# Four of w_out's eight pieces requested behind the store of w_sp's halves, and converted behind the last theta

## The chip, the cores and the metric

The kernel runs on one core of one Trainium2 chip. The metric is the device time of one execution in microseconds (us), lower is better. Times shown as "median of runs" are of repeated executions; a profiled execution is a further one, from which all rows of the trace come.

## The reference, cut to what matters

Three blocks follow one another on an activation of 4 batches x 576 positions x 512 channels, all in float32:

```python
# 1. windowed attention, 8 heads: softmax(scale * q k^T + mask) v           -> x [4, 576, 512]
# 2. mixing
theta = x @ w_theta                                  # 512 x 512
zr, zi = x * cos(theta), x * sin(theta)
u = x + w_tok_r @ zr + w_tok_i @ zi                  # over the 576 positions
x2 = u + relu(u @ w_ch)
# 3. gated MLP
h = relu(x2 @ w_in); hu, hv = h[..., :512], h[..., 512:]
v_s = w_spatial @ layernorm(hv) + b_spatial          # over the 576 positions
out = (hu * v_s) @ w_out                             # w_out is 512 x 512
```

The weights are handed in as float64; products are made in pairs of float32r numbers ("h" and "l", the rounded value and the rest), so each weight must be converted and split before it is used. `w_out` is needed by the last product only.

## The kernel before, in words

TensorE (PE) holds three matmuls for every product (h with h, l with h, h with l). Work is staged by batch: attention of batch b+1 and the mixing of batch b run side by side, then the gated MLP runs batch by batch. The names used below:

- `th_run(3, ...)` is theta of the last batch (its sines on ScalarE (ACT), its products on VectorE (DVE), its split `zl` on GpSimd (POOL)). `tm_run(b, ks)` is the token mixing of a batch; each of its eight steps ends in a DVE addition at line 553, which is kept in the list `mixed`; `uh` and `ul` are its split sums (ACT and POOL). `ch_run(b)` is the product with `w_ch`; it ends each group in a DVE operation at line 574, which frees a PSUM bank, and in a store `x2d<-x`.
- Float64 weights arrive in pieces in the ring `w64` of the pool `stg`, which has four slots. A piece of 256 columns is converted by five instructions: ACT line 141 (`w64g<-w`), DVE line 142 (`c<-w`, into the PSUM tile `c64`), DVE line 143, the rounded half by DVE line 120 (`parts<-w64g`) and the rest by POOL line 176. Lines 141 and 142 are the last to read the slot. SyncE (SP) then stores the pair to a DRAM buffer with line 177.
- `j_out` lists w_out's eight pieces (load with line 170, conversion as above, store to `wo_d`). `wo_load` reads all of them back (line 822) for the output products.
- `w_gate(0)` and `w_gate(1)` load two pieces of `w_sp` each (lines 757 and 758) into the same ring, take **two more slots of it** for sums (`c` from line 761 on, `d` from line 764 on), and split four tiles (ACT line 767, DVE line 768). They are called `a`, `b`, `c` and `d` in the text, and `a'` to `d'` in the second call.
- `w_half()` converts the last 64 rows of `w_sp` and ends in the two stores at line 244 (`wh_d<-wsph`).
- `first_parts` (line 731) splits sums of batch 0's activation on ACT and POOL (`x2tl<-first,x2th`); `x2s`, and lines 859 to 868, are the first steps of the MLP.

The order of the work is made by a planner before the run. It walks through a modelled timeline; whenever an engine is free, it takes, of the instructions whose inputs are planned and whose tile can have a slot, the one that stands first in the program. Loads are instructions of SP's queue for it. Each engine then runs its list in that order, waiting at each instruction for its inputs. `tc.issue_after(ins)` says that what is traced inside may only stand behind `ins` on the engine of `ins`; it holds back nothing on other engines, and it makes no wait. `behind(list, f)` does that for each instruction of a list. `late(pairs, lag, last)` requests a piece per step, and lets the conversion follow two steps later, behind `last()`:

```python
def late(pairs, lag, last):
    ...
            load, finish = todo.pop(0)
            waiting.append((finish, load()))
        if len(waiting) > lag or not todo:
            finish, st = waiting.pop(0)
            behind(last(), lambda: finish(st))
```

So a load of `late` is held by nothing, and a conversion by the step of the token mixing at which it is called (on DVE, since `mixed` holds DVE instructions). Before the change all eight pieces of `j_out` run through it, spread over `tm_run(3, K_ALL)` at 1.25 calls per step: conversions are called at steps 3, 4, 4, 5, 6, 7, 8 and 8. At the same place the second half of `w_gate(0)` is called at step 4, and the loads and the second half of `w_gate(1)` at steps 5 and 6.

Of the kernel before, what the change touches and what calls it, by code (L numbers as in the profile page):

```python
# [47 lines left out]
LAG_W = 2  # L48
SECOND_RATE = 1.5
OUT_RATE = 1.25  # L50
CH_BEFORE = 4
PE_MASK = 1
PAIR = 2
HELD = 2
SP_FIRST = 5


# [7 lines left out]
K_ALL = (8,) + K_MAIN  # L65
# [3 lines left out]
def tile_block(ctx: ExitStack, tc: tile.TileContext, qT, kT, vw, eye_in, mask_in, eye_b_in, w_theta, w_tok, w_ch, w_in, w_sp, w_sph, b_sp, w_out, out):  # L69
    nc = tc.nc  # L70
    V, A, G, PE, SY = nc.vector, nc.scalar, nc.gpsimd, nc.tensor, nc.sync

    def f32(ap):
        return ap.bitcast(F32)
# [18 lines left out]
    wh_d = dram.tile([P, 2, 3 * CH], F32R, name="wh_d")  # L93
# [102 lines left out]
    def gate_half(kk):  # L196
# [14 lines left out]
        def add(blk, x, y, z, op):  # L211
            def finish(_):
                V.tensor_tensor(g[x], g[y], g[z], op=op)
                out(blk, g[x])
            return (lambda: None), finish
# [2 lines left out]
        return [read(0, 0, 0), read(1, 0, None), read(0, 1, 1), read(1, 1, 2),  # L218
                add(3, a22, a21, a22, ALU.add), add(5, a21, a11, a21, ALU.subtract), add(4, a11, a22, a11, ALU.subtract), add(6, a12, a12, a11, ALU.subtract)]

    def w_half():
        (st, bt), (hh, lb) = ([patt.tile(sh, d, tag=t, name="wsph", bufs=2) for _ in range(2)] for sh, d, t in (([P, S + WIN], F32, "k"), ([P, NT, P], F32R, "v")))
        hh, lb = (t.rearrange("p t k -> p (t k)")[:, :3 * CH] for t in (hh, lb))
        sd = stg.tile([P, CH], F32, tag="stage", name="stage", bufs=4)
        bd = stg.tile([P, CH], F32, tag="stage", name="stage", bufs=4)

        def load():
            SY.dma_start(st[:, :S], w_sph)
            for r in (64, 96):
                SY.dma_start(bt[r:r + 1, :S], b_sp)  # L230

        def finish(_):
            V.tensor_tensor(sd, st[:, :CH], st[:, CH:S], op=ALU.subtract)
            G.memset(f32(lb[HALF:]), 0.0)
            for r in (64, 96):
                V.tensor_tensor(bd[r:r + 1], bt[r:r + 1, :CH], bt[r:r + 1, CH:S], op=ALU.subtract)
            for s_, b_, c in ((st[:, :S], bt[:, :S], slice(0, S)), (sd, bd, slice(S, 3 * CH))):
                A.copy(hh[:, c], s_)
                V.tensor_tensor(lb[:HALF, c], s_[:HALF], f32(hh[:HALF, c]), op=ALU.subtract)
                for r in (64, 96):  # L240
                    A.copy(lb[r:r + 1, c], b_[r:r + 1])
                V.tensor_tensor(lb[96:97, c], b_[96:97], f32(lb[96:97, c]), op=ALU.subtract)
            for i, t in enumerate((hh, lb)):
                SY.dma_start(f32(wh_d[:, i]), f32(t))

        return load, finish

# [188 lines left out]
    zlast = {}  # L436
    x_cast = []
    mixed = []
# [3 lines left out]
    def split(dst_h, dst_l, src, eh="a", el="g"):  # L442
        copy(dst_h, src, eh)
        return (G if el == "g" else V).tensor_tensor(dst_l, src, f32(dst_h), op=ALU.subtract)  # L444
# [68 lines left out]
    def th_shared(b):  # L513
        th_unit(b, 4, True)
        yield

    def th_run(b, ts):
        for t in ts:
            th_unit(b, t)
            yield  # L520

    def u_tiles(b):
        if b not in uu:
            uu[b] = tuple(p1.tile([P, 4, S], F32R, tag=n, name=n) for n in ("uh", "ul"))
        return uu[b]

    def tm_run(b, ks, last=True):

        if last:
            uh, ul = u_tiles(b)  # L530
        for c in range(2):
            cs = slice(CH * c, CH * (c + 1))

            early = b == 0 and c == 0
            accs = []
            for d in range(4):
                if early and d < 2:
                    if d == 0:
                        accs = [ps_mm.tile([P, 512], F32, tag="mm", name="ps_y") for _ in range(2)]
                        for i, k in enumerate(ks):  # L540
                            for e in range(2):
                                for j, (lh, rh) in enumerate(((zh, wtok_h), (zl, wtok_h), (zh, wtok_l))):
                                    PE.matmul(accs[e][:, :CH], lh[b, k][:, P * e:P * (e + 1)], rh[:, k, cs], start=(i + j == 0), stop=(i == len(ks) - 1 and j == 2))
                    ps = accs[d]
                else:
                    ps = ps_mm.tile([P, 512], F32, tag="mm", name="ps_y")
                    n = 0
                    for k in ks:
                        for lh, rh in ((zh, wtok_h), (zl, wtok_h), (zh, wtok_l)):
                            PE.matmul(ps[:, :CH], lh[b, k][:, P * d:P * (d + 1)], rh[:, k, cs], start=(n == 0), stop=(n == 3 * len(ks) - 1))  # L550
                            n += 1
                xv = x[b][:, d, cs]
                mixed.append(V.tensor_tensor(xv, ps[:, :CH], xv, op=ALU.add))
                if last:
                    x_cast.append(split(uh[:, d, cs], ul[:, d, cs], xv, "a", "g"))
                yield
# [3 lines left out]
    def ch_run(b):  # L560

        uh, ul = uu.pop(b)
        wch_h, wch_l = wch
        for c in range(2):
            cs = slice(CH * c, CH * (c + 1))
            for e in range(4):
                ps = ps_mm.tile([P, 512], F32, tag="mm", name="ps_r")
                n = 0
                for k in range(4):
                    for lh, rh in ((wch_h, uh), (wch_l, uh), (wch_h, ul)):  # L570
                        PE.matmul(ps[:, :CH], lh[:, k, P * e:P * (e + 1)], rh[:, k, cs], start=(n == 0), stop=(n == 11))  # L571
                        n += 1
                xv = x[b][:, e, cs]
                finished[:] = V.scalar_tensor_tensor(xv, ps[:, :CH], 0.0, xv, op0=ALU.max, op1=ALU.add),  # L574
                SY.dma_start(x2d[b][:, e, cs], xv)
                yield

    def run(gen):
        for _ in gen:
            pass  # L580

    def spread(main, *fills):

        acc = [0.0] * len(fills)
        for _ in main:
            for i, (gen, rate) in enumerate(fills):
                acc[i] += rate
                while acc[i] >= 1.0:
                    acc[i] -= 1.0
                    next(gen, None)  # L590
        for gen, _ in fills:
            run(gen)

    def jobs(fns):
        for f in fns:
            f()
            yield

    def take(gen, n):
        for _ in range(n):  # L600
            yield next(gen)

    def chain(*gens):
        for g in gens:
            yield from g
# [6 lines left out]
    j_out = [stored(w_out[:, k, H2 * c:H2 * (c + 1)], wo_d[:, k, :, H2 * c:H2 * (c + 1)]) for c, k in cols]  # L612

    def late(pairs, lag, last):

        waiting = []
        todo = list(pairs)
        while todo or waiting:
            if todo:
# [5 lines that stand above are left out]
            yield  # L625
# [7 lines left out]
    def behind(ins, f):  # L633

        with ExitStack() as st:
            for i in ins:
                st.enter_context(tc.issue_after(i.ins))
            f()
# [26 lines left out]
    tm = tm_run(PAIR, K_MAIN, False)  # L665
    spread(take(tm, 7 - HELD), (attention(PAIR + 1), ATT_RATE_PAIR))
    for i in range(HELD):
        with tc.issue_after(values[12 * (PAIR + 2) - HELD + i].ins):
            next(tm)
    spots.clear()  # L670
    run(late([w_half()], LAG_W, last_softmax))
    run(th_shared(PAIR))
    th = th_run(PAIR + 1, (0, 1, 2, 3))
    next(th)

    with tc.issue_after(turned[PAIR + 1, 0].ins):
        run(tm)
    spread(th, (chain(tm_run(PAIR, (8,)), ch_run(PAIR)), TAIL_RATE))
    patt.release()
    ps_t.release()  # L680
    pth.release()
# [89 lines left out]
    def x2_held():  # L771
        for _ in range(2):
            behind([mixed[-1], x_cast[-1]], lambda: next(x2_first))
            yield
# [14 lines left out]
    x2_first = x2_load(0)  # L789
    next(x2_first)  # L790
    gw = gate_weights()
    spread(tm_run(3, K_ALL), (chain(take(gw, 1), x2_held(), gw, jobs([first_sums])), 1.0), (late(j_out, LAG_W, lambda: mixed[-1:]), OUT_RATE))
    pz.release()
    p2s = tc.alloc_tile_pool(name="p2s", bufs=1, side="right", reuse_waits="tile")
    win_u = [p2s.tile([P, 7, 2, H2], F32R, name=f"winu{n}") for n in "hl"]
# [295 lines left out]
    for pr in (0, 2):  # L1091
# [5 lines left out]
        sp, load = sp_run(b0), x2_load(b1)  # L1097
        next(load)
        run(take(sp, SP_FIRST))
        with tc.issue_after(aside[-1].ins):  # L1100
# [82 lines left out]
```

## Time and profile before

| what | value |
|---|---|
| median of 3 runs | 529.14 us (528.4 to 529.62) |
| the profiled execution's own time | 528.77 us |
| span of its trace | 527.0 us |
| PE busy | 509.9 us, 97% of the span |
| DVE, ACT, POOL busy | 362.9, 294.8, 211.4 us |

Time outside the span is 1.77 us. "Busy" is a share over the whole span; what one stage is worth is read from that stage's rows. In the rows an idle time in brackets, or behind "<-", names what the engine waited for last. PEclk is the TensorE clock that was granted, as a share of 2.4 GHz.

### The profile page before, as it was taken

How to read it: one execution, taken by the hardware profiler on the slowest of the kernel's cores; microseconds unless marked ns; L12 is line 12 of the kernel's file. 1: busy time of each engine (PE TensorE's matmuls, PEld its weight loads, DVE VectorE, ACT ScalarE, POOL GpSimd, SP SyncE). 2: the span in 40 equal slices, each digit the busy share in tenths (PEclk: the TensorE clock that was granted, in tenths of full speed). 3: DMA queues.
4: the chain of work that ended last, by engine and by line, in shares of the span. 5: the costliest groups of instructions: out<-in, count | busy, mean ns of one | idle time of the engine just before them, and what ended most of it. 6: DMA issues, size and time to landing. Idle time of an engine off the chain costs nothing. (4 is left out here: it accounts for less than half of the span.)

```text
span 527.0 us, 10548 instructions
## 1 busy us (share of the span) xinstructions
PE 509.9 (97%) x3764; PEld 468.2 (89%) x3764; DVE 362.9 (69%) x895; ACT 294.8 (56%) x825; POOL 211.4 (40%) x264
## 2 busy tenths in 40 slices
PE   5979999999999999999999998999999999999997
PEld 5857899987999989999899997999899889988996
DVE  2888999576645757564762799787964939699350
ACT  4879875637777567674770344345454445355332
POOL 3875986427645537230394346203201400140040
PEclk9989999999999999999999998999999999999999
DMA  8986387681257941421017369722012030301003
GB/s 234 339 275 189 83 241 228 201 292 63 70 152 210 298 152 57 114 70 69 1 45 235 101 193 363 242 105 91 21 62 90 2 119 2 91 0 61 22 1 101
DMA packets 59481, 69.60 MB, mean 132 GB/s; under 512 B 25282, under 2 KB 42178, under 8 KB 59172
## 3 DMA queue, kind: packets, MB, share of 16 engines
q1 hardware_dynamic: 57204, 68.37, 41.3%
q10 hardware_dynamic: 2224, 0.55, 0.5%
q8 instruction: 30, 0.49, 0.4%
q14 instruction: 23, 0.19, 0.1%
HBM read 50.72 MB, written 18.19 MB: 131 GB/s over the span
## 5 line engine op out<-in xcount | busy, mean ns | idle before, releaser
L444 POOL TENSOR_TENSOR gl<-hu,gh 128x288 fp32r<-128x288 f32 (+1 forms) x32 | 30.2, 954 | 145.5 <-ACT gh L118 124.9
L550 PE MATMUL ps_y<-wtok_h,zh 128*128 128x288 f32 x270 | 81.3, 303 | 1.0 <-DVE sm L373 0.9
L550 PE MATMUL ps_y<-wtok_l,zh 128*128 128x288 f32 x270 | 80.2, 297 | 0.0
L550 PE MATMUL ps_y<-wtok_h,zl 128*128 128x288 f32 x270 | 80.2, 298 | 0.0
L550 PEld LDWEIGHTS ps_y<-wtok_h,zh 128*128 128x128 f32 x270 | 50.5, 188 | 1.9 <-DVE sm L373 1.2
L550 PEld LDWEIGHTS ps_y<-wtok_h,zl 128*128 128x128 f32 x270 | 50.7, 188 | 0.3
L550 PEld LDWEIGHTS ps_y<-wtok_l,zh 128*128 128x128 f32 x270 | 50.7, 188 | 0.2
L380 POOL TENSOR_TENSOR sm<-sm,l 128x288 f32<-128x288 f32 x48 | 32.3, 675 | 43.0 <-DVE l L379 33.6
L377 ACT ACTIVATE sm<-sm,m 128x96 f32<-128x96 f32 x108 | 39.1, 364 | 7.3 <-DVE m L374 5.9
L571 PE MATMUL ps_r<-uh,wch_h 128*128 128x288 f32 x128 | 38.7, 304 | 2.5 <-DVE r L861 1.3
L571 PE MATMUL ps_r<-ul,wch_h 128*128 128x288 f32 x128 | 37.8, 301 | 0.6 <-POOL ul L444 0.6
L571 PE MATMUL ps_r<-uh,wch_l 128*128 128x288 f32 x128 | 38.2, 299 | 0.0
L444 POOL TENSOR_TENSOR ul<-x,uh 128x288 fp32r<-128x288 f32 x32 | 28.1, 885 | 21.7 <-ACT uh L118 21.0
L361 PE MATMUL s<-kt,qz 128*128 128x96 f32 x252 | 36.2, 283 | 0.0
L361 PEld LDWEIGHTS s<-kt,qz 128*128 128x128 f32 x252 | 34.0, 202 | 0.7
L942 PE MATMUL ps_sp<-wsp_h,vl 128*128 128x288 f32 x112 | 32.7, 295 | 0.0
L176 POOL TENSOR_TENSOR parts<-w64g,parts 128x256 fp32r<-128x256 f32 x22 | 17.9, 818 | 36.2 <-DVE parts L120 33.0
L942 PE MATMUL ps_sp<-wsp_l,vh 128*128 128x288 f32 x112 | 32.4, 294 | 0.0
L942 PE MATMUL ps_sp<-wsp_h,vh 128*128 128x288 f32 x112 | 32.2, 296 | 0.0
L141 ACT ACTIVATE w64g<-w 128x256 f32<-128x256 f32 (+1 forms) x46 | 19.7, 443 | 19.6 <-DMA w<-w_in 9.7
L472 PE MATMUL ps_th<-wth_h,xh 128*128 128x512 f32 (+1 forms) x76 | 30.6, 403 | 0.0
L472 PE MATMUL ps_th<-wth_h,xl 128*128 128x512 f32 (+1 forms) x76 | 30.0, 395 | 0.4 <-DVE xl L467 0.3
(231 smaller groups left out, 1602.2 us busy)
## 6 DMA issues: line engine op xcount, KB each, us to landing
vt<-vw SPq DMA_DIRECT2D x15, 576.0 KB, 6.2
x2d<-x SPq DMA_DIRECT2D x32, 144.0 KB, 3.0
kt<-kT SPq DMA_DIRECT2D x15, 304.0 KB, 4.4
w<-w_in SPq DMA_DIRECT2D x16, 256.0 KB, 3.9
w<-w_tok SPq DMA_DIRECT2D x14, 288.0 KB, 4.4
out<-o SPq DMA_DIRECT2D x15, 256.0 KB, 2.0
qz<-qT SPq DMA_DIRECT2D x26, 144.0 KB, 4.7
x2tl<-x2d SPq DMA_DIRECT2D x6, 576.0 KB, 4.9
```

The costliest lines, as they stand in the source:

```text
L141: A.activation(g, hw.bitcast(F32), AF.Prelu, scale=2.0**-112, alpha=2.0**32)
L176: G.tensor_tensor(t[:, 1], src, f32(t[:, 0]), op=ALU.subtract)
L361: PE.matmul(s[:, KW * blk:KW * (blk + 1)], qz[:, t].rearrange("p j q -> p (j q)"), kt[:, T * t:T * t + KW], start=not on_pe, stop=not on_pe)
L377: ia = A.activation(sm[:, t, :], src[:, t, :], AF.Exp, bias=m_[:, t:t + 1], scale=scale, accum_out=ls[:, t, 0:1])
L380: ig = G.tensor_tensor(sm, sm, l.unsqueeze(2).to_broadcast([P, 3, KW]), op=ALU.mult)
L444: return (G if el == "g" else V).tensor_tensor(dst_l, src, f32(dst_h), op=ALU.subtract)
L472: PE.matmul(ps, lh[:, k, :], rh[:, k, :], start=(i == 0), stop=(i == 11))
L550: PE.matmul(ps[:, :CH], lh[b, k][:, P * d:P * (d + 1)], rh[:, k, cs], start=(n == 0), stop=(n == 3 * len(ks) - 1))
L571: PE.matmul(ps[:, :CH], lh[:, k, P * e:P * (e + 1)], rh[:, k, cs], start=(n == 0), stop=(n == 11))
L942: PE.matmul(ps[:, :CH], a[i][kk], b[j][kk], start=start, stop=(kk, j) == (1, 1), skip_group_check=True)
```

## The change

The first four pieces of `j_out` leave the list that is spread over `tm_run(3)`. Their loads are called behind the second store of w_sp's halves on SP, ahead of the last theta in the program; their conversions are called behind the last ACT, DVE and POOL instruction of batch 3's theta. The other four pieces stay in `late`, which now begins with them: conversions are called at steps 3, 4, 4 and 5 of the token mixing. The number of instructions and of bytes is the same.

```diff
+EARLY_OUT = 4
...
+    halves_out = []
+
     def w_half():
...
-                SY.dma_start(f32(wh_d[:, i]), f32(t))
+                halves_out.append(SY.dma_start(f32(wh_d[:, i]), f32(t)))
...
     run(late([w_half()], LAG_W, last_softmax))
+    with tc.issue_after(halves_out[-1].ins):
+        loaded = [(finish, load()) for load, finish in j_out[:EARLY_OUT]]
     run(th_shared(PAIR))
...
     spread(th, (chain(tm_run(PAIR, (8,)), ch_run(PAIR)), TAIL_RATE))
+    for finish, st in loaded:
+        behind(zlast[PAIR + 1], lambda: finish(st))
     patt.release()
...
-    spread(tm_run(3, K_ALL), (chain(take(gw, 1), x2_held(), gw, jobs([first_sums])), 1.0), (late(j_out, LAG_W, lambda: mixed[-1:]), OUT_RATE))
+    spread(tm_run(3, K_ALL), (chain(take(gw, 1), x2_held(), gw, jobs([first_sums])), 1.0), (late(j_out[EARLY_OUT:], LAG_W, lambda: mixed[-1:]), OUT_RATE))
```

## Rows read from the trace of the kernel before

**Rows 1.** What PE waited for, between 240 and 340 us.

```profile
PE ps_r L571 <- DVE r L861: 1.3, 1, 1.3
PE ps_r L571 <- POOL ul L444: 0.6, 1, 0.6
```

**Rows 2.** The chain that ended last: start, us, work.

```profile
325.18 3.07 PE ps_r L571 x12
328.25 3.03 PE ps_hv L852 x12
331.28 3.20 PE ps_r L571 x24
334.48 5.46 PE ps_hv L852 x24
```

**Rows 3.** Three stretches: busy us of PE, PEld, DVE, ACT, POOL; PEclk, DMA share, GB/s.

```profile
281.00:292.00 11.00, 11.00 (x86) 11.00 (x85) 1.72 (x4) 1.76 (x3) 1.61 (x2) 1.00 0.94 318
311.50:322.50 11.00, 11.00 (x68) 10.02 (x67) 11.00 (x16) 7.51 (x13) 8.47 (x8) 1.00 0.90 311
325.20:329.20 4.00, 4.00 (x16) 3.82 (x17) 3.29 (x14) 1.09 (x4) 0.00 (x0) 0.57 1.02 354
```

**Rows 4.** DVE's timeline: start, us, operation, idle time before it.

```profile
292.03 0.42 DVE L142 TENSOR_SCALAR c<-w 128x256 uint32<-128x256 uint32 x1
...
299.75 0.45 DVE L761 TENSOR_TENSOR w<-w 128x288 f32<-128x288 f32 x1
...
305.15 0.45 DVE L764 TENSOR_TENSOR w<-w,w 128x288 f32<-128x288 f32 x1
...
311.46 0.46 DVE L761 TENSOR_TENSOR w<-w 128x288 f32<-128x288 f32 x1 [0.25 <-DMA w<-w_sp]
...
317.67 1.99 DVE L768 TENSOR_TENSOR wsp_l<-w,wsp_h 128x576 fp32r<-128x576 f32 x1
...
324.68 0.42 DVE L574 SCALAR_TENSOR_TENSOR x<-ps_r,x 128x288 f32<-128x288 f32 x1
```

**Rows 5.** DVE's groups between 311.46 and 325.1 us: busy, mean ns.

```profile
L768 DVE TENSOR_TENSOR wsp_l<-w,wsp_h 128x576 fp32r<-128x576 f32 (+1 forms) x4 | 5.2, 1295 | 0.0
...
L120 DVE CAST parts<-w64g 128x256 fp32r<-128x256 f32 x2 | 1.4, 724 | 0.0
```

**Rows 6.** POOL's timeline: the splits of `x2t` beside those groups.

```profile
315.05 1.69 POOL L444 TENSOR_TENSOR x2tl<-first,x2th 128x576 fp32r<-128x576 f32 x1 [2.53 <-ACT x2th L118]
...
317.61 4.82 POOL L444 TENSOR_TENSOR x2tl<-first,x2th 128x576 fp32r<-128x576 f32 x3
```

**Rows 7.** SP's timeline: loads into the ring, and the halves' stores.

```profile
174.84 0.34 SPq L757 DMA_DIRECT2D w<-w_sp  x1
175.97 0.59 SPq L758 DMA_DIRECT2D w<-w_sp  x1
177.28 0.57 SPq L170 DMA_DIRECT2D w<-w_out  x1
178.57 0.62 SPq L170 DMA_DIRECT2D w<-w_out  x1
...
242.59 2.48 SPq L244 DMA_DIRECT2D wh_d<-wsph  x2
292.47 0.34 SPq L170 DMA_DIRECT2D w<-w_out  x1
...
308.02 0.33 SPq L758 DMA_DIRECT2D w<-w_sp  x1
```

**Rows 8.** The pieces' conversion after 270 us: ns min/median/max, first and last start.

```profile
L143 DVE SCALAR_TENSOR_TENSOR w64g<-w64g,c x8: 409/410/421, 293.6 to 331.4; 128x256 uint32<-128x256 uint32 x8
L120 DVE CAST parts<-w64g x8: 277/285/1171, 296.8 to 335.1; 128x256 fp32r<-128x256 f32 x8
L176 POOL TENSOR_TENSOR parts<-w64g,parts x8: 736/848/1167, 297.2 to 335.4; 128x256 fp32r<-128x256 f32 x8
L141 ACT ACTIVATE w64g<-w x6: 427/436/443, 295.4 to 330.3; 128x256 f32<-128x256 f32 x6
```

## The prediction

> **What bounds the kernel now.** PE is busy for 97% of the span (the table above), so I read first what PE waits for. Between 240 and 340 us there are just two waits, 0.6 and 1.3 us, both ahead of groups of `ch_run(3)`: one for a POOL split `ul`, one for DVE [rows 1]. That is 1.9 us of idle PE. The chain that ended last shows what comes behind it: 12 matmuls of `ps_r` took 3.07 us from 325.18, whereas 24 of the same took 3.20 us from 331.28, so 12 should take 1.60; 12 of `ps_hv` took 3.03 us where half of 5.46 is 2.73 [rows 2]. The loss is 1.47 + 0.30 = 1.8 us, and the windows name it: right behind the wait the granted clock is 0.57, between the levels 1.2 and 2.4 GHz, while it is 1.00 in the stretch before [rows 3]. The wait and the clock together cost 1.9 + 1.8 = 3.7 us. Nothing else in this part of the kernel can be won, since PE is busy all through the other two stretches [rows 3].
>
> Why does DVE come late? The wait ends with the 0.42 us operation of line 574 at 324.68, which frees the bank [rows 4]. From 311.5 to 322.5 DVE has no idle time (11.00 of 11.00), against 1.72 of 11.00 between 281 and 292 [rows 3]. Its unbroken run begins at 311.46, when the data of `w_gate(1)` land [rows 4]. Inside it stand the second gate's four splits, 5.2 us, and two rounded halves of pieces of w_out, 1.4 us [rows 5]. They are dear because POOL works beside them: its splits of `x2t` run from 315.05 and, three in a row, from 317.61 for 4.82 us [rows 6]; a split of line 768 takes 1.99 us there [rows 4] against a mean of 1.30 [rows 5].
>
> **The change part by part.** *The loads.* Four loads go behind the halves' stores, which are issued at 242.59 and take 2.48 us of SP's queue [rows 7]. On SP they would pass the stores of `x2d` and the loads of `winv` and `first`; that costs four issues of some 0.6 us where SP mostly waits. But do they get a slot? The ring has four. Before, `a` and `b` of the first gate were requested at 174.84 and 175.97, and two pieces at 177.28 and 178.57; the third piece came only at 292.47 [rows 7], 0.02 us behind line 142, which began at 292.03 and took 0.42 us [rows 4]. So the ring is full from 178.6 to 292.45, and the planner fills it with any load that nothing holds. After the change the four early loads are held behind 242.59, but the four pieces left in `late` are not: two of them should take the slots at 177.28 and 178.57. Then the early loads find no slot at 245, and the first of them is issued near 292.5. What the change then does is another thing than it says: it swaps the pieces. Up to 292 us nothing changes.
>
> *The conversions.* A piece costs ACT 0.44, DVE 0.42 + 0.41 + 0.28 and POOL 0.74 us when nothing is in the way, up to 1.17 for line 120 and for line 176 [rows 4, 8]. Eight remain eight. The early four stand first in the program, so DVE takes them whenever they have landed, and the unheld four are called at steps 3, 4, 4 and 5, not 3 to 8. So all eight come ahead of the late part of the gates; before, the last ones ran as late as 335.1 [rows 8]. ACT's and POOL's parts are hidden by the same slack as before. No wait on a semaphore is added beyond the data's; the loads' issue behind the store and the conversions' behind theta are order alone.
>
> *What it takes out of the stretch.* In DVE's run from 311.46 stand two operations of line 120 (1.45), two of line 143 (0.82) and one of line 142 (0.42): 2.69 us [rows 4, 5, 8]. I leave one piece there, 1.11 us. That takes 1.58 us away from in front of line 574.
>
> *What it puts in.* The first gate needs two more slots, `c` for line 761 at 299.75 and `d` for line 764 at 305.15 [rows 4]. Of the loads that stand before them in the program there are now five that wait: the early four and the third unheld one. A slot turns in about 3.9 us: 3.44 from the issue at 308.02 [rows 7] to the landing at 311.46, and 0.42 for line 142 [rows 4]. One slot opens at 292.45, 296.3, 300.2 and 304.0; the other, which `c` took at 299.75, opens then, at 303.6 and at 307.5. Five loads use the first five openings, `c` gets that of 304.0 and `d` that of 307.5, which is 2.3 us later than 305.15. The second gate's loads, which take the slots of the first, are late by as much, or by nothing if landings are quicker than this one. Bounds: 0 and 2.3; no row lies between, so I take the middle, 1.2. Who waits for the second gate? Only DVE's own queue, as its weights are used later, in the `ps_sp` products; but what stands behind it on DVE is line 574.
>
> *The sum.* 1.2 - 1.58 = -0.4 us on the wait of 1.9; PE still waits, and the clock still falls. 528.77 - 0.4 = 528.4 for the profiled execution, which lies 0.4 below the median of the runs; so 528.7 against 529.14.
>
> One rule speaks against moving conversions to 276 to 281, where POOL splits `zl`. The Trainium skill (GPSIMD Engine Reference, 1. Specifications) says that GpSimd shares its SBUF interfaces with VectorE, in contention with instructions that have two SBUF inputs or run in a two-port mode. The trace agrees: 1.99 us for a two-input split beside POOL [rows 4]. By that rule the four operations of line 120 could cost 1.17 each in place of 0.28, 3.6 us in all, and the sum would stay as it is, for DVE has 9.3 us idle from 281 to 292 [rows 3].
>
> **The rivals.** *A. The same swap, but PE's wait goes.* With the last pieces out of the crowded stretch, line 574 comes in time. For it: 1.58 us are taken out, POOL's `ul` (0.6 of the wait) loses a split of line 176 ahead of it, and if the second gate isn't late the wait of 1.9 shrinks to some 0.3, too little, perhaps, for the clock to fall. Against it: the slots above. Price: from -1.6 (the wait alone) to -3.7 (with the clock): 525.4 to 527.5.
>
> *B. Slower: the second gate falls into POOL's splits.* If its loads land 3.6 us later, at 315.05 where POOL begins [rows 6], its four splits run at 1.99, not 1.30: 4 x 0.69 = 2.8 us more. Then 3.6 + 2.8 - 1.6 = +4.8 at the most, 533.9; less where POOL is done before DVE (its three end at 322.4), by about half, +2.4: 531.5. It decides from a delay of some 2.6 us on (2.6 - 1.6 = 1.0), so from a landing behind 314.1. For it: SP runs in order, and a store that waits for a conversion holds the loads behind it. Against it: it needs more than the 2.3 us found above. The rule of the Trainium skill named above (GPSIMD Engine Reference, 1. Specifications) bears on this rival, and the trace agrees with the 1.99 us.
>
> *C. The loads do come at 245.* If the planner leaves the ring's slots for them, all four land by 250 and are converted from 276 to 292, where DVE, ACT and POOL are busy for 1.72, 1.76 and 1.61 of 11 us [rows 3] and need 4.4, 1.8 and 3.0 more. The crowded stretch loses its pieces, and the whole 3.7 goes: 525.4. Against it: nothing holds the other four back, as nothing held the first two at 177.28.
>
> **How the numbers follow.** A difference under 0.2%, 1.06 us, is about what a measurement of this kernel can't tell from none. Chances: the forecast (swap, between -1 and +1 us) 0.32; A 0.27; B 0.29; C 0.12. Faster: A's 0.27 and 0.11 of C, 0.38. Same: the forecast and 0.01 of C, 0.33. Slower: B, 0.29. The forecast's own range is 527.6 to 529.9 (its bounds of 0 and 2.3 us give -1.6 and +0.7). Cases of both signs hold most of the chance, so the range reaches from the whole gain, 529.14 - 3.7 = 525.4, to 532.0, a little past B's half; B's worst stays out.
>
> **What would show it.** Right: SP issues `w<-w_out` at about 177 and 178 and not again before 292; all eight conversions end before 316; line 761 of the first gate comes near 304, the second gate's first operation between 311.5 and 314; PE waits at about 322 to 325 for 1 to 2 us, and a granted clock under 1 follows. Wrong: loads of `w_out` at 245 and DVE busy between 281 and 292 (C), no wait of PE and a clock of 1.00 through 330 (A), or a wait of 3 us and more with splits of line 768 near 2 us behind 318 (B). The likeliest error is in how the planner deals out the slots, since no row shows it with other pieces waiting.

## The result, and the profile after

The changed kernel takes 531.58 us (median of 20 runs, 528.54 to 535.84), the kernel before 528.57 (20 runs, 526.81 to 530.52): a ratio of 1.0062, 95% interval 1.0046 to 1.0078. By the ratio it is slower by 3.3 us, by the medians by 3.0. Its lines stand one to seven further down than before: line 757 is 764 here, 764 is 771, 768 is 775, 120 is 121.

SP's timeline of the changed kernel (start, us on the queue) answers to [rows 7]:

```profile
243.92 2.48 SPq L247 DMA_DIRECT2D wh_d<-wsph  x2
246.44 2.10 SPq L171 DMA_DIRECT2D w<-w_out  x4
274.55 3.04 SPq L578 DMA_DIRECT2D x2d<-x  x4
278.03 0.33 SPq L764 DMA_DIRECT2D w<-w_sp  x1
279.44 0.33 SPq L765 DMA_DIRECT2D w<-w_sp  x1
...
281.33 0.33 SPq L171 DMA_DIRECT2D w<-w_out  x1
...
282.48 0.33 SPq L171 DMA_DIRECT2D w<-w_out  x1
...
284.59 1.00 SPq L178 DMA_DIRECT2D wo_d<-parts  x1
...
287.27 2.69 SPq L795 DMA_DIRECT2D first<-x2d  x2
290.05 5.40 SPq L178 DMA_DIRECT2D wo_d<-parts  x2
295.56 0.54 SPq L171 DMA_DIRECT2D w<-w_out  x1
...
311.69 0.38 SPq L764 DMA_DIRECT2D w<-w_sp  x1
312.85 0.33 SPq L765 DMA_DIRECT2D w<-w_sp  x1
```

The early four do load at 246.44. The four loads that stood at 174.84 to 178.57 in [rows 7] are gone from there: the ring takes no load between 163 and 246.44. The first gate's two loads and two pieces of w_out come only when the early four have left their slots, at 278.03 to 282.48, among the stores of `x2d`, ahead of `winv` and of `first`, which is issued at 287.27.

ACT's timeline shows when `first` has landed, as `x2h` is its first use:

```profile
298.84 1.16 ACT L119 CAST x2h<-first 128x1152 fp32r<-128x1152 f32 x1 [3.77 <-DMA first<-x2d]
300.44 1.16 ACT L119 CAST x2h<-first 128x1152 fp32r<-128x1152 f32 x1 [0.44 <-DMA first<-x2d]
```

In the kernel before, ACT's timeline has the same two casts 6 to 8 us earlier:

```profile
291.10 1.16 ACT L118 CAST x2h<-first 128x1152 fp32r<-128x1152 f32 x1 [2.08 <-DMA first<-x2d]
...
294.37 1.15 ACT L118 CAST x2h<-first 128x1152 fp32r<-128x1152 f32 x1 [1.78 <-DMA first<-x2d]
```

DVE stands behind them in its own order, as its timeline shows (start, us, idle time before it in brackets; it answers to [rows 4]):

```profile
278.53 0.52 DVE L121 CAST parts<-w64g 128x256 fp32r<-128x256 f32 x1
...
293.94 0.29 DVE L121 CAST parts<-w64g 128x256 fp32r<-128x256 f32 x1 [4.08 <-DMA wo_d<-parts]
...
300.03 1.36 DVE L447 TENSOR_TENSOR x2l<-first,x2h 128x1152 fp32r<-128x1152 f32 x1 [4.56 <-ACT x2h L119]
...
304.46 0.99 DVE L768 TENSOR_TENSOR w<-w 128x288 f32<-128x288 f32 x1
...
310.78 0.44 DVE L771 TENSOR_TENSOR w<-w,w 128x288 f32<-128x288 f32 x1
...
315.53 1.01 DVE L768 TENSOR_TENSOR w<-w 128x288 f32<-128x288 f32 x1
...
317.53 1.98 DVE L775 TENSOR_TENSOR wsp_l<-w,wsp_h 128x576 fp32r<-128x576 f32 x1
319.44 1.51 DVE L121 CAST parts<-w64g 128x256 fp32r<-128x256 f32 x1
320.87 0.45 DVE L556 TENSOR_TENSOR x<-ps_y,x 128x288 f32<-128x288 f32 x1
...
322.73 4.17 DVE L775 TENSOR_TENSOR wsp_l<-w,wsp_h 128x576 fp32r<-128x576 f32 x3
...
328.24 0.42 DVE L577 SCALAR_TENSOR_TENSOR x<-ps_r,x 128x288 f32<-128x288 f32 x1
```

The two idle times before 293.94 and 300.03 are 8.6 us in which DVE has nothing to do, with both gates still ahead of it. They are two different waits. The one of 4.56 us is for `first`. The one of 4.08 us is for a place to put a converted piece: the pool `parts` has two buffers, and the store to `wo_d` that frees the one it needs is issued at 284.59, between the two loads of `winv`, and lands 9.2 us later. The windows put the idle time in one number (busy us of PE, PEld, DVE, ACT, POOL; PEclk, DMA share, GB/s; the first answers to [rows 3]):

```profile
281.00:292.00 11.00, 11.00 (x86) 11.00 (x85) 3.33 (x9) 2.30 (x5) 3.98 (x5) 1.00 0.91 283
...
292.00:304.00 12.00, 12.00 (x93) 12.00 (x92) 5.39 (x10) 3.62 (x5) 3.73 (x5) 1.00 0.67 235
304.00:313.00 9.00, 9.00 (x70) 9.00 (x69) 9.00 (x16) 2.48 (x5) 3.48 (x4) 1.00 0.23 77
313.00:324.00 11.00, 7.98 (x49) 7.09 (x49) 11.00 (x18) 7.19 (x14) 8.15 (x7) 1.00 0.91 311
324.00:330.00 6.00, 4.84 (x30) 4.29 (x29) 5.63 (x13) 1.55 (x3) 2.58 (x2) 1.00 1.00 367
```

From 292 to 304 us DVE is busy for 5.39 of 12 us. The kernel before has 10.48 there, and 7.78 of 9 in the next stretch, as its windows show:

```profile
292.00:304.00 12.00, 12.00 (x93) 12.00 (x92) 10.48 (x20) 4.09 (x8) 5.05 (x5) 1.00 0.15 46
304.00:313.00 9.00, 9.00 (x68) 8.95 (x67) 7.78 (x17) 2.59 (x6) 3.95 (x5) 1.00 0.67 209
```

So DVE has 1.6 us more done between 281 and 292, then 5.1 less, and has no pause from 304 on (9.00 of 9, 11.00 of 11). What stands at the end of that run is late, and POOL works beside it, as its timeline shows (it answers to [rows 6]):

```profile
317.31 3.48 POOL L447 TENSOR_TENSOR x2tl<-first,x2th 128x576 fp32r<-128x576 f32 x2 [1.09 <-ACT x2th L119]
...
321.72 3.59 POOL L447 TENSOR_TENSOR x2tl<-first,x2th 128x576 fp32r<-128x576 f32 x2
```

PE's waits between 240 and 345 us are 4.2 us where they were 1.9 [rows 1]:

```profile
PE ps_r L574 <- DVE x L556: 3.0, 1, 3.0
PE ps_r L574 <- DVE r L868: 1.2, 1, 1.2
```

The longer one is for line 556 (before: line 553), the last addition of the token mixing, which begins at 320.87 behind a dear split and a dear cast. In the kernel before DVE's timeline has it 6.6 us earlier:

```profile
314.32 0.45 DVE L553 TENSOR_TENSOR x<-ps_y,x 128x288 f32<-128x288 f32 x1
```

This profiled execution took 530.63 us. One execution can't be set against another by its end: the halves' store starts anywhere from 242.37 to 245.86 us in the 20 profiles of this study, and here 1.3 us later than in [rows 7]. These differences stand before 153 us already, ahead of every load that the change moves: from the load of `vt` near 154 us to the store it is 89.2 to 89.5 us in all 20. So times below are also counted from that store ("t0").

### The profile page after: what moved, and what is told of

It reads as the page before. It is cut to its first block, busy times and chain, and to the rows that moved or that the text cites. A ratio compares the mean times of both kernels' runs of the same rounds, so it can differ in the third digit from the quotient of the medians.

```text
span 528.8 us, 10547 instructions
## 1 busy us (share of the span) xinstructions
PE 507.6 (96%) x3764; PEld 465.8 (88%) x3764; DVE 364.2 (69%) x895; ACT 294.8 (56%) x825; POOL 211.9 (40%) x264
## 5 line engine op out<-in xcount | busy, mean ns | idle before, releaser
L447 POOL TENSOR_TENSOR gl<-hu,gh 128x288 fp32r<-128x288 f32 (+1 forms) x32 | 31.3, 989 | 146.1 <-ACT gh L119 95.5
L447 POOL TENSOR_TENSOR ul<-x,uh 128x288 fp32r<-128x288 f32 x32 | 26.6, 839 | 20.6 <-ACT uh L119 19.9
L574 PEld LDWEIGHTS ps_r<-uh,wch_h 128*128 128x128 f32 x128 | 24.0, 188 | 6.7 <-DVE x L556 3.3
```

## The experiments

Two theories. **Slots**: the planner deals out the ring's slots in the order of the program, so that the early four, which stand first and are held behind 242 us, keep the whole ring empty until then; the displaced loads then fall on the stretch before `first`, and both gates come late on DVE. **Conversions**: the work itself, moved beside theta, costs more there than it saves. Within the first, it was open which late thing costs: `first`, the gates, or the splits beside POOL. Each time below is the median of 11 or 12 runs unless another number is given, set against the kernel before on the same chip; edits of their own shift the line numbers by a few again.

**e1: the early four in places of their own.** Their loads go to two buffers that are no longer in use (`qzero`) in place of the ring:

```diff
-        loaded = [(finish, load()) for load, finish in j_out[:EARLY_OUT]]
+        loaded = []
+        for i, k in enumerate(range(EARLY_OUT)):
+            st = qzero[i // 2]...[:, DM * (i % 2):DM * (i % 2 + 1)]...
+            SY.dma_start(st, w_out[:, k, :H2].bitcast(U32))
+            loaded.append((j_out[k][1], st))
```

> The changed kernel, but its four early loads go into the two zero-padded query tiles (free after the last attention) and not into the ring w64; all else as changed. Theory 1 (the ring): the early four keep all four slots from 175 to 277 us, which pushes the first gate's two loads and the next two pieces of w_out from 175 to 179 to 278 to 282.5, in front of winv and first, so that first lands some 6 us late. Here the ring is free, so these four loads are back at 175 to 179, first lands near 292 to 295, and the time is that of the kernel before or below it (-3 to +0.5 us). Theory 2 (the moved conversions' own stores and the two slots of parts): they stay, so the time stays 2.5 to 3.3 us above before. Theory 3 (the second gate, late for want of slots): the slots c and d come as before, so between -1 and +1.

528.81 us, ratio 0.9991 (0.9971 to 1.0011): the loss is gone. SP's timeline (without the stores of line 178 that stand between these loads) shows the displaced loads back at their old time, and the early four still behind the halves:

```profile
177.04 0.34 SPq L768 DMA_DIRECT2D w<-w_sp  x1
...
178.17 0.58 SPq L769 DMA_DIRECT2D w<-w_sp  x1
...
179.47 0.58 SPq L171 DMA_DIRECT2D w<-w_out  x1
...
180.78 0.57 SPq L171 DMA_DIRECT2D w<-w_out  x1
...
247.30 2.12 SPq L679 DMA_DIRECT2D qz<-w_out  x4
```

So it was the slots. The wait for `parts` is there in e1 as well, on DVE's timeline, so by itself it does not make the loss:

```profile
290.93 0.29 DVE L121 CAST parts<-w64g 128x256 fp32r<-128x256 f32 x1 [3.78 <-DMA wo_d<-parts]
```

**e8: the same slots, not held** (`with nullcontext():` in place of the `issue_after`).

> The changed kernel without the hold behind the halves' stores: the four early loads may go as soon as the ring has slots (near 175 to 179). They still stand first in the program and keep the slots until their conversion behind theta, so the first gate's loads and the next two pieces still come at 278 to 283 (theory 1): as the changed kernel, +2.3 to +3.5 us against before. If it's the loads' own traffic at 246 that costs, as before.

532.77 us (6 runs), 1.0076 (1.005 to 1.0103). The early four load at 176.40 to 180.13, and the first gate's loads are issued at 278.36 and 279.69 as in the changed kernel. So the holding is not what costs; who has the slots is.

**e2: only the displacement.** The kernel before, with the ring's first four loads held behind stores of `x2d`, where the change puts them:

```diff
+        with nullcontext() if kk else tc.issue_after(x2_store[8 * PAIR + 3].ins):
             SY.dma_start(a, w_sp[:, kk])
             SY.dma_start(b, w_sp[:, kk + 2])
...
+        with tc.issue_after(x2_store[8 * PAIR + 5].ins) if len(x2_store) >= 24 else nullcontext():
             SY.dma_start(st[:, :DM], src.bitcast(U32))
```

> The kernel before, with no early piece at all, but the first gate's loads held behind the fourth x2d store of batch 2's w_ch product and the first two pieces of w_out behind the sixth, about where the changed kernel has them. Theory 1: this alone makes first late and costs most of the loss, +1.5 to +3.3 us against before, with PE waiting longer at 320 to 326. Theory 2: no early conversion and no early store, so as before within 0.7 us. Theory 3: c and d come from the same slots as before, so as before or up to +1.

531.01 us, 1.0041 (1.0014 to 1.0067): two thirds of the loss by the middle of the interval, without any early conversion. `x2h` begins 53.1 us behind t0, before 48.5, in the changed kernel 54.9.

**e3 and e4: `first` ahead of `winv`.** If the transfers ahead of `first` are what makes the gates late, the 2 MB of `winv` can go behind it: e3 in the changed kernel, e4 in the kernel before.

```diff
...
+    with tc.issue_after(first_dma.ins):
+        for i, t in enumerate(win_v):
+            SY.dma_start(f32(t), f32(win_d[:, :, i]))
```

> The changed kernel, with the two loads of winv (2 MB, not used until some 315 us) held behind the two loads of first on SP. If what costs is that first lands late (theories 1 and 2), first lands 5 us or more sooner than the 298.8 and 300.4 of the changed kernel, DVE's idle time of 4.6 us in front of the split x2l goes, and the loss shrinks to between -1 and +1.5 us. Theory 3 alone: the second gate's loads still come late (near 312), so the loss stays at 2.5 to 3.3.

> The kernel before, with winv held behind first. If first's landing is what paces DVE from 291 on, DVE's wait of 1.5 us for x2h at 294 goes, its backlog at 311 to 325 shrinks, and the 1.9 us of PE's wait with its clock loss are won in part: -0.5 to -3 us. If the second gate's loads alone set the backlog (theory 3): no change within 0.7 us.

e3: 529.40 us, 1.0006 (0.9981 to 1.003); e4: 527.63, 0.9970 (0.9947 to 0.9993). It takes some 3 us from the changed kernel and 1.6 from the one before, so about half of that gain comes in either kernel.

**e9: only `first` late.** The kernel before with `winv` loaded twice:

```diff
-    for i, t in enumerate(win_v):
...
+    for i, t in enumerate(win_v * 2):
...
```

> The kernel before, with winv loaded twice, the second copy of its first half between winv and first: the ring's loads, the pieces and the gates are as before, only first lands some 3 to 5 us later behind 1 MB more. If first's landing is what the change spoils, this costs +1.5 to +3 us by itself. If what costs is the gates' or the pieces' own late loads, as before within 0.7 us.

529.11 us, 1.0006 (0.9987 to 1.0026). `x2h` begins 51.8 and 53.5 us behind t0 where it began 48.5 and 51.8, but DVE takes the first gate meanwhile (55.6 behind t0) and is busy for 10.34 of 12 us from 292 to 304. So `first` by itself, 3.2 and 1.7 us late, costs nothing that these runs can tell from none (the interval reaches from -0.7 to +1.4 us). That this is because DVE has a gate to work on is my reading. In the changed kernel `first` is later still, by 6.4 and 4.7 us, and no run has that alone.

**e5 and e12: only the second gate late.** Its two loads in the kernel before, held behind a store to `wo_d`; in e12 behind the fourth such store and called two steps later (the lines shown are e12's; its change to the call is left out).

```diff
+        with tc.issue_after(kept_dma[-2].ins) if kk else nullcontext():
             SY.dma_start(a, w_sp[:, kk])
             SY.dma_start(b, w_sp[:, kk + 2])
```

> The kernel before, with the second gate's two loads held behind the third store to wo_d: first and the first gate come as before, only the second gate's data land some 3 us later (near 314 to 315, where POOL's splits of x2t begin). If the second gate's lateness is the last link by which first's lateness costs (theory 1's chain), this alone costs +1 to +3 us, with PE waiting longer on DVE near 323. If first's lateness costs by another way, the time is as before within 0.7 us.

> The kernel before, with the second gate's two loads called two steps later and held behind the fourth store to wo_d, so that its data land at 315 to 318 and its splits fall into POOL's splits of x2t, with first and the first gate as before. If the second gate's lateness costs (my rival B): +1 to +3 us, PE waiting longer near 322 to 328. If not, as before within 0.7 us.

e5 missed its aim: the gate's first operation came 0.4 us later behind t0 than before, and the time stayed (528.77 us, 1.0007, 0.9988 to 1.0026). e12 moved it from 68.9 to 73.4 us behind t0, by 4.5 (the changed kernel by 2.7, and by 4.7 in its second profile, e10): 531.98 us (8 runs), 1.0061 (1.0039 to 1.0083). PE's waits and a window of e12:

```profile
PE ps_r L572 <- DVE x L575: 3.7, 1, 3.7
```

```profile
324.00:330.00 6.00, 2.25 (x11) 2.02 (x10) 5.87 (x16) 2.40 (x4) 1.60 (x2) 0.81 1.03 422
```

So a second gate that is late alone can cost as much as the whole change. But it does so by other waits than rival B's and than the changed kernel's. DVE's timeline of e12:

```profile
314.70 0.45 DVE L554 TENSOR_TENSOR x<-ps_y,x 128x288 f32<-128x288 f32 x1
...
321.82 2.60 DVE L770 TENSOR_TENSOR wsp_l<-w,wsp_h 128x576 fp32r<-128x576 f32 x2
...
325.24 0.95 DVE L770 TENSOR_TENSOR wsp_l<-w,wsp_h 128x576 fp32r<-128x576 f32 x1
...
327.31 0.43 DVE L770 TENSOR_TENSOR wsp_l<-w,wsp_h 128x288 fp32r<-128x288 f32 x1
```

The gate's four splits take 3.98 us here, less than the 5.2 of the kernel before, so they are late and not dear. And the last addition of the mixing, at 314.70, is 70.6 us behind t0, before 71.7, whereas the changed kernel has it at 77.0 and waits for it longest.

**e6 and e17: POOL's splits of `x2t` on DVE**, in the changed kernel and in the one before:

```diff
-            split(h, l, s, "a", "g")
+            split(h, l, s, "a", "v")
```

> The changed kernel, with the four low halves of x2t subtracted on DVE and not on POOL: DVE gets four more operations of some 0.75 us, and no POOL operation with two inputs runs beside the second gate. If the dear splits there (2.0 us in place of 0.75) come from POOL's work, they fall to some 0.75, and the time falls by 1 to 2.5 us against the changed kernel, to +1 to +2 against before. If they come from the DMA traffic, they stay dear, DVE is longer by 3 us and more, and the time is +5 or more.

> The kernel before with the low halves of x2t on VectorE, as e6 has them in the changed kernel. If e6 came back to 1.0001 because the second gate's splits no longer meet POOL's: here 0.998 to 1.002, since the second gate lands in time before and has less to lose. If the move by itself gains about 3 us in any kernel: 0.993 to 0.996, and e6 says nothing of the loss.

e6: 528.66 us, 1.0001 (0.9969 to 1.0033), with the second gate still 70.8 us behind t0. DVE's timeline of e6 shows what its splits cost with POOL away:

```profile
315.53 0.75 DVE L775 TENSOR_TENSOR wsp_l<-w,wsp_h 128x576 fp32r<-128x576 f32 x1
...
321.57 1.78 DVE L775 TENSOR_TENSOR wsp_l<-w,wsp_h 128x576 fp32r<-128x576 f32 x3
```

2.53 us for four, against 6.15 in the changed kernel. Taken alone, e6 seems to explain the whole loss. e17 says otherwise: the same edit makes the kernel before faster too, 526.49 us, 0.9973 (0.9952 to 0.9994). Of e6's gain of 0.6 to 0.7%, 0.27% comes in either kernel; the rest, somewhat over half of the loss, is what the splits beside POOL cost on account of the change. With the intervals of three ratios in it, that share can be anything from none to all.

**e7, e10, e11: repeats.** e7 and e11 are both repairs together (e1 and e3), e10 is the changed kernel again.

> Both repairs at once: the early four in the query tiles (e1) and winv behind first (e3). Theory 1: first lands near or ahead of its place before, half of w_out's conversions lie in DVE's idle time at 277 to 292, and PE's wait at 322 to 326 is short or gone: -1.5 to -3.7 us against before, faster than e1 and than e4. Rival: the early pieces' stores and conversions give nothing, and this is as e4 alone (-1.5).

> The changed kernel once more, for its time on the same chip beside the others of this call and for a second profiled execution: +2.5 to +3.5 us against before; PE waits for DVE by 3 us or more in all between 318 and 330, and in this execution its granted clock may fall behind the wait, which it did not in the first one.

> The kernel with both repairs once more, since its profiled execution had no wait of PE and lay at 525.97 us while its median did not differ from before. If the repair holds in every execution, the median is 1 to 3 us below before; if the other executions lose elsewhere, again no difference.

e7: 528.77 us, 0.9991 (0.9968 to 1.0015); e11: 529.35, 0.9994 (0.9972 to 1.0016); e10: 532.97 (8 runs), 1.0071 (1.0047 to 1.0096). The two repairs together do not gain what e4 gains alone, which spoke for a part of the **Conversions** theory. e7's profile has no wait of PE between 240 and 345 us and takes 525.97 us; e11's, of the same kernel, has 2.8 us of waits. The first difference that I found between the two is one cast on DVE, here from the timelines of DVE and of POOL in e10, where it is the same:

```profile
278.34 3.62 DVE L121 CAST parts<-w64g 128x256 fp32r<-128x256 f32 x1
```

```profile
279.26 1.30 POOL L447 TENSOR_TENSOR zl<-tb,zh 128x512 fp32r<-128x512 f32 x1
280.51 1.30 POOL L447 TENSOR_TENSOR zl<-ta,zh 128x512 fp32r<-128x512 f32 x1
```

The first of the early casts ends at 281.96, when POOL's splits of `zl` end (281.81). In e11 it is 3.62 us again; it took 0.54 in e7, and 0.52 in the first profile of the changed kernel, above.

**e13 and e14: the early four's cast on ACT**, with both repairs and in the changed kernel alone:

```diff
-        behind(zlast[PAIR + 1], lambda: finish(st))
+        behind(zlast[PAIR + 1], lambda: finish(st, "a"))
```

> Both repairs as in e7 and e11, and the early four's first conversion step (the rounded half) on ScalarE instead of VectorE. If the conversions on VectorE (3.62 us for the first of them in e11, beside POOL's pair) are what takes back the gain of the two repairs: no VectorE operation over 1.5 us at 275 to 282 us, ratio 0.994 to 0.998 (1 to 3 us below before), and a narrower spread. If they are not the cause: 0.998 to 1.002 again, with times from 526 to 532 us.

> The changed kernel with only the early four's rounded halves on ScalarE. If VectorE's conversions are part of the loss: the loss falls from 3.3 us to 1 to 2.5. If the loss comes from the second gate's late loads alone: 2.5 to 3.5 us above before, x2h and the second gate's loads as late as in the changed kernel.

e13: 527.19 us (525.46 to 529.52), 0.9971 (0.9951 to 0.9992); e14: 530.56, 1.0039 (1.0015 to 1.0062). By the ratios both are 1.1 to 1.7 us better than the same kernel with the cast on DVE; each difference alone lies just inside its uncertainty (0.2% on 0.25%), the two together outside. The edit does two things at once: it takes the cast off DVE, and it takes DVE's waits for `parts` away (4.08 us above, and 1.66 before the cast ahead of that one), which stand on ACT in e14. No run parts the two. e13's runs span 4.1 us where e7's and e11's span about 6. e13's profile has no wait of PE between 240 and 345 us, and its clock stays up in the stretch that answers to the third of [rows 3]:

```profile
324.00:330.00 6.00, 6.00 (x39) 5.52 (x38) 3.28 (x12) 0.98 (x3) 0.00 (x0) 1.00 1.03 398
```

**e15, e16 and e18: what is left to gain.** e15 is e1 with the cast on ACT; e16 is e4 again on the same chip; e18 is e4 with e17's edit.

> The change with the early four in places of their own (as e1) and their rounded halves on ScalarE (as e13), first and winv in the order of before. If the early conversions gain once they neither hold the ring nor cast on VectorE: as far below before as e13, ratio 0.995 to 0.998. If e13's gain is that of first ahead of winv alone (as in e4): 0.999 to 1.001.

> The kernel of e4 once more, on the chip of e15: the kernel before with first ahead of winv. If the gain of e4 holds: 0.995 to 0.999. If it was chance: 0.999 to 1.001.

> The kernel before with first ahead of winv (e4) and the low halves of x2t on VectorE. If the two gains are of one wait, no more than e4 alone: 0.996 to 0.999. If VectorE's splits beside POOL cost time of their own: 0.992 to 0.995, the fastest version here.

e15: 528.22 us, 0.9982 (0.9968 to 0.9997); e16: 527.18, 0.9965 (0.9949 to 0.9981); e18: 525.95, 0.9956 (0.9938 to 0.9974), the fastest here. With places of its own and the cast on ACT, the change gains 0.8 us; beside `first` ahead of `winv` it gains nothing (e13 0.9971, e16 0.9965). PE's only wait in e16 between 240 and 345 us:

```profile
PE ps_r L571 <- DVE r L862: 1.0, 1, 1.0
```

## Why the prediction was wrong, point by point

**What bounds the kernel: right in place, too large in size.** The end is set by PE's waits on DVE at 320 to 330 us, as [rows 1, 2] said. The 3.7 us to be won were those of one execution. Counted from t0, the profile before takes 286.2 us, e13's 283.1 and e16's 283.7; the medians of the best versions without a new placement of the `x2t` splits lie 1.5 to 1.9 us below before. Executions of the kernel before range from 525.88 to 534.56 us, so presumably not all of them pay both the wait and the clock.

**The loads: the step that failed.** "The planner fills it with any load that nothing holds [...]. After the change the four early loads are held behind 242.59, but the four pieces left in `late` are not: two of them should take the slots at 177.28 and 178.57." They don't. No load of the ring passed the early four, whether they were held (246.44) or not (176.40, e8), and with places of their own for them the others were back at 177 (e1). So the early four have all four slots from the first, and until 246.44 the ring stands empty. That the planner deals out slots in the order of the program is read off these runs. I took the four loads at 175 to 179 in [rows 7] for those that happened to be free to go, but they are also the first four in the order of the program, with which the row agrees as well. "Up to 292 us nothing changes" fell with it: before 292 stand the displaced loads.

**The conversions.** All eight casts on DVE do come early, between 278.53 and 319.44, and from the second gate's first operation on two operations of pieces are left, 1.92 us where I had left 1.11: the last cast cost 1.51 us there and not 0.28.

**What it puts in.** I had `c` near 304 and `d` near 307.5; they came at 304.46 and 310.78, so the first looks right and is so for another reason: not slots that turned late, but the first gate's own loads and `first` that came late, and DVE idled for 8.6 us. The second gate was to begin between 311.5 and 314, and began at 315.53. The turn of a slot was misread besides: 3.44 us runs from the issue of `b'` to the first use of `a'`, which was issued at 306.58. The trace has 4.8 us from issue to landing for `a'` and 4.1 for `b'`. With 4.1 + 0.42 for a turn, the same openings put `d` near 308.8, an estimate: 3.6 us late in place of 2.3, which is the delay that rival B asked for.

**The sum.** -0.4 us forecast, +3.0 in the medians (+3.3 by the ratio). The two profiles don't show that difference: from t0 the kernel before takes 286.2 us and the changed one 286.7. PE's waits went from 1.9 to 4.2 us, but the clock, which cost 1.8 us before, stayed at 1.00. The changed kernel's second profile, e10, takes 291.3 us from t0, with 5.6 us of waits between 240 and 345 and a clock of 0.84 from 330 to 341. What the sum lacked is the place of the wait: I let only line 574 stand behind the second gate on DVE, but the last addition of the mixing came to stand behind its first split, 5.2 us later from t0 than before, and PE waited 3.0 us for it.

**Rival B had the outcome.** Its sign, a wait of 3 us behind 318 us with a split near 2 us, was seen in the main, and its price, 531.5 us, was met; that it fits to 0.1 us is luck. Its mechanism was half of it: the four splits cost 6.15 us beside POOL against 5.2 in [rows 5], 1.0 more where it had 2.8, and the second gate began 4.07 us later, of which 2.7 are left when counted from t0. That a second gate late by 4.5 us can cost as much is shown (e12), by another wait; that POOL's splits carry a part of the loss is likely, its size is open (e6 against e17). The change makes the first gate late as well (60.5 us behind t0, before 57.2), and no run here parts the two gates in the changed kernel. **Rival C had the cause:** the loads came at 246.4 to 248.5 us, DVE's free time from 281 to 292 was used (3.33 us, before 1.72), but the rest of its chain took for granted that the other loads stayed where they were.

**The casts beside theta.** I let four of them cost 1.17 us each at the most and called that hidden. One took 3.62 us in two profiles of eight (e10, e11), three times the nearest row's 1.17. The Trainium skill (GPSIMD Engine Reference, 1. Specifications) says that GpSimd shares its SBUF interfaces with VectorE, in contention with instructions of two SBUF inputs or in a two-port mode. The trace agrees as far as the cast ended with POOL's splits (281.96 and 281.81); the cast has one input, and no run here shows whether it ran in a two-port mode. Taking the casts off DVE, and its waits for `parts` with them, is worth 1.1 to 1.7 us in two kernels (e13, e14); the 0.5 in a third (e15 against e1) can't be told from none.

**Still open.** Why 3.62 us in one execution and 0.52 in another of the same kernel: in both the cast begins 0.3 us before a one-input operation of POOL. And which of the late things costs in the changed kernel: `first` with the first gate, the second gate, or the mixing's last addition behind it.

## What to carry to other kernels

A load that is called early takes its ring slot in the order of the program, not of time, whether it is held or not: before moving one ahead, list who had those slots, and follow the displaced loads to the stretch in which they will run. Idle time of an engine that is busy for 69% of the span was followed here by a run without pauses, up to the step that PE waits for, and by a loss of 3 us: read idle time by what comes behind it. And an edit that undoes a loss has shown its cause only by what it gains beyond its gain in the kernel before.

## What the runs showed that I had not expected

- A cast of 128x256 on DVE took 3.62 us beside POOL's two-input splits, 0.52 in another execution of the same kernel, and 0.28 at its quickest [rows 8].
- The clock does not follow the length of a wait: it stayed at 1.00 from 324 to 330 us behind a wait of 3.0 us in the changed kernel, and was 0.72 on average in the same stretch of the kernel before, whose longest wait is 1.3, and 0.81 in e12 with 3.7, both between the levels of 1.2 and 2.4 GHz.
- Four splits of `x2t` moved from POOL, which is busy for 40% of the span, to DVE at 69% made the kernel before 1.9 us faster by the medians (e17). DVE's own splits of 128x576 took 0.75 to 1.15 us there, where one had taken 1.99 [rows 4].
